# A token-mixing MLP block on one core: the first two tiles of x in one load, 64 words of w1 read on the second ring, and a new order of the work

## Chip, core and metric

The kernel runs on one core of one Trainium2 chip. The metric is the device time of one execution in microseconds (us). The median of four runs stands for the kernel. The profile is of one more execution; it lists the core's engines: PE (TensorE, matrix products; PEld is its weight load), DVE (VectorE), ACT (ScalarE), POOL (GpSimd) and SP (SyncE, which only issues DMAs here).

## What is computed

One batch, S = 2048 tokens, D = 512 features, F = 1792, all in bf16:

```python
h = _gelu(_layernorm(x, axis=-1) @ w1)                 # w1: 512 x 512
c = D // 4
g0 = ...   # the first quarter of h's columns, one token later
g1 = ...   # the second, one token earlier
g2 = ...   # the third, two tokens later
g3 = ...   # the fourth, two tokens earlier
hs = jnp.concatenate([g0, g1, g2, g3], axis=-1) @ w2   # w2: 512 x 512
x1 = x + hs
h2 = _gelu(_layernorm(x1, axis=-1) @ w3) @ w4          # w3: 512 x 1792, w4: 1792 x 512
return x1 + h2
```

Tokens that a shift would take from outside the sequence count as zero.

## The kernel before

The tokens are cut into 16 tiles of 128. All of x, x1 and the weights stay in on-chip memory. A tile passes through these steps:

- **Load.** `load` issues x by tiles (`x3`, or `x4-5` for two tiles in one DMA), w1, w2 and w4 in halves (`w1a`, `w1b`) and w3 whole. The order is the string `LOADS`. Everything goes on SP's queue, but for `x0@act`, which ScalarE issues on its own queue. Besides loads, SP's queue carries the DMA transposes (line 463) and 15 of the stores of the output.
- **Layernorm of layer 1** (`ln`). Mean and variance come from VectorE (lines 416 and 418) or, for tiles in `STAT_ACT`, from two passes on ScalarE (lines 395 and 400) and small VectorE steps. GpSimd raises the variance to the power -1/2 (`rstd`, line 423). The normalized tile is written by the engine that `NORM` names, VectorE by default (line 445), ScalarE (454) or GpSimd (457); for the last two a product of mean and rstd is made first (`nmr`, line 450, on the engine that `NMR` names).
- **Transpose.** Matrix products need features on partitions. Tiles in the script's `sa`, `sb` and `ty` steps are transposed on TensorE (line 490) and copied out of its accumulators (line 498) by the engines that `EVAC` names; the others by a DMA transpose on SP's queue. Numbers of 16 and above in `ty` and `tp` mean the second layernorm of tile number minus 16.
- **up1** with w1 and gelu (lines 626 and 641). Tiles are taken in groups, `GROUPS[1]`; `up1:6` in the script is group 6, not tile 6.
- **mix** (line 666): four products of shifted columns of h with w2 for one tile, then x1 on VectorE (lines 673, 677). Tile t needs h of tiles t-1 to t+1.
- **Layernorm of layer 2**, transposes, **up2** with w3 and gelu by groups `GROUPS[2]` (tiles 0-1, 2-5, 6-9, 10-11, 12-15), **down** with w4 (line 695), sum and store (lines 703 and 706).

Tile 0 takes a short way (`NAT`, `SPLIT`): only its mean is subtracted before the product (line 431, in two halves); it is turned in two halves (`sa`, `sb`), multiplied row-wise by the two halves of w1 (`ra` needs w1a, `rb` needs w1b; line 528), and scaled by rstd inside its gelu (line 569). The result is turned back (`th`, line 594) and copied (line 604).

TensorE's order is written out by hand in `SCRIPT`. `warm:9` at its head is nine products of zeros (line 720). Each other engine's order comes from a planner in `Program.order` and `Program.place`: each step gets a due time, counted back from TensorE's list, and at each moment the engine takes, of the steps that the planner holds ready, the one due first. `DUE` is where the count starts, `LAG` adds to the planned landing of loads and transposes, and `BIAS` moves single steps' due times by hand. The loads on a queue keep the order of `LOADS`. `emit` writes the instructions in the planned order and adds semaphore waits for true dependencies; instructions that the planner starts before `ENTRY` are moved ahead of the program's opening barrier.

```python
LOADS = """
x1 x2 tp2 x0@act w1a w1b x3 x4-5 tp5 w2a w2b x6-7 w3 tp17 w4a x8-10 w4b tp6 x11-12 tp1 tp16 x13-15
"""
```

Entries `tp` in `LOADS` that TensorE transposes are skipped; of these only `tp6` remains.

Of the kernel before, what the change touches and what calls it, by code (L numbers as in the profile page):

```python
# [6 lines left out]
P = 128  # L7
ACT_F = mybir.ActivationFunctionType
ALU = mybir.AluOpType
BF16 = mybir.dt.bfloat16  # L10
# [15 lines left out]
class Program:  # L26
# [2 lines left out]

    HOP = {"pe": 200.0, "dve": 155.0, "act": 220.0, "pool": 120.0, "sp": 70.0}  # L30
    LOOK = {"dve": 300.0, "act": 300.0}
    DUE = 164483.0
    BEGIN = {"sp": 30.0, "act": 150.0, "pe": 400.0, "dve": 150.0, "pool": 450.0}
    ENTRY = 1900.0
    COLD, RESTART = 4300.0, 800.0
    LAG = {"load": 750, "tp": 700}

    def __init__(self):
        self.ops = []
# [12 lines left out]
    def order(self):  # L52
# [58 lines left out]
        assert seen == len(self.ops), "cycle"  # L111
        if self.DUE:

            topo, left = [], [len(d) for d in preds]
            stack = [i for i, n in enumerate(left) if n == 0]
            while stack:
                i = stack.pop()
                topo.append(i)
                for j in succs[i]:
                    left[j] -= 1  # L120
                    if left[j] == 0:
                        stack.append(j)
            due, t = {}, self.DUE
            for op in self.ops:
# [12 lines left out]
        for op in self.ops:  # L137
            op.prio += BIAS.get(op.name, 0.0)
            if op.first is not None:
# [11 lines left out]
    def place(self, succs, order_only):  # L151
# [46 lines left out]
        def land(op):  # L198
            nonlocal moved, last
            if op.queue == "tp":  # L200
                at = max(clock + 500.0, op.start + 2450.0, last + 600.0) + self.LAG["tp"]
            elif op.name.startswith("out"):
                at = clock + 300.0
                self.total = max(self.total, at)
            else:
                moved += op.dur
                at = clock + 600.0 + min(600.0, 0.3 * moved) + (600.0 if op.dur > 1400.0 else 0.0)
                at += self.LAG["load"] if moved > 1200.0 else 50.0
            if op.queue != "tp":
# [47 lines left out]
        self.seq = out  # L257
        return out

GROUPS = {1: (1, 1, 1, 1, 2, 1, 4, 2, 2, 1), 2: (2, 4, 4, 2, 4)}  # L260
NORM = {0: "act", 3: "act", 7: "pool", 8: "act", 9: "pool", 10: "pool", 11: "pool", 12: "pool", 14: "act", 15: "act", 16: "pool", 18: "act", 19: "act", 24: "pool", 25: "act", 26: "pool", 27: "pool", 29: "pool", 30: "pool", 31: "act"}
EVAC = {0: "both", 1: "both", 2: "both", 4: "both", 8: "both", 9: "dve", 10: "dve", 11: "dve", 12: "dve", 13: "dve", 14: "dve", 16: "dve", 17: "dve", 19: "both", 20: "both", 21: "both", 22: "both", 23: "both", 24: "dve", 25: "both", 27: "both", 29: "both", 30: "both", 31: "both"}
STAT_ACT = (0, 7, 9, 12, 13, 15, 18, 21, 25, 29, 30)
TAIL = (256, 160, 96)
NMR = {0: "pool", 1: "pool", 3: "pool", 5: "pool", 6: "pool", 7: "pool", 8: "pool", 9: "pool", 11: "pool", 13: "pool", 14: "pool", 15: "pool", 16: "pool", 17: "pool", 18: "pool", 20: "pool", 21: "pool", 22: "pool", 26: "pool", 27: "pool", 28: "pool", 29: "pool", 31: "pool"}
NAT = (0,)
SPLIT = (0,)
CSPLIT = ()
HEV = {0: "dve", 4: "dve"}
BIAS = {}  # L270
LOADS = """
x1 x2 tp2 x0@act w1a w1b x3 x4-5 tp5 w2a w2b x6-7 w3 tp17 w4a x8-10 w4b tp6 x11-12 tp1 tp16 x13-15
"""
SCRIPT = """
warm:9 sa:0 sb:0 ty:1 ra:0 rb:0 ty:2 up1:1 th:0 up1:2 mix:0 ty:3 ty:5 mix:1 ty:4 up1:3-4 ty:16 mix:2 ty:17
mix:3 up2:0 mix:4 up1:5 down:1 down:0 mix:5 up1:6-7 mix:8 mix:6 up1:9 mix:9-10 up1:8 mix:7 mix:11 up2:1
mix:13 mix:15 up2:3 down:5 mix:12 up2:2 mix:14 down:2 down:4 down:3 down:6-8 down:11 down:9 up2:4 down:10
down:12-15
"""

def bass_standalone__mixer_s_mlp__prompt_kernel(nc, x, w1, w2, w3, w4, out):
# [3 lines left out]
    NT, DC, FC = S // P, D // P, F // P  # L285
    groups = {l: [(sum(GROUPS[l][:i]), n) for i, n in enumerate(GROUPS[l])] for l in GROUPS}
    NXN, NO, NPAIR, NOB, NJ = 16, 4, 3, 2, 4
# [8 lines left out]
    with ExitStack() as es:  # L296
        sb = lambda name, shape, dt: es.enter_context(nc.sbuf_tensor(name, shape, dt))
# [22 lines left out]
        warm = sb("warm", [P, 1], F32)  # L320
# [6 lines left out]
        pg = Program()  # L327
# [56 lines left out]
        def ln(layer, t):  # L384
# [3 lines left out]
            col = lambda a: a[:, q : q + 1]  # L388
            how = NORM.get(q, "dve")
            sign = -1.0 if q in NAT and how == "act" else 1.0  # L390
            if q in STAT_ACT:
                if layer == 1:
# [22 lines left out]
            else:  # L415
# [4 lines left out]
                       writes=[(("mv", q), 0), (("vpe", q), 0)], dur=75)  # L420
            var = vpe[:, q : q + 1] if q in STAT_ACT else mv[:, q, 1:2]
            pg.add("pool", f"rstd{q}",
# [3 lines left out]
            if q in NAT:  # L426
                assert how != "act" or q in STAT_ACT

# [18 lines left out]
            else:  # L447
                eng = NMR.get(q, "dve")
                pg.add(eng, f"nmr{q}",
# [17 lines left out]
        def pe_transpose(t, q, pair):  # L467
            layer = 1 if q < NT else 2
            how = EVAC.get(q, "act")
            if pair:  # L470
# [104 lines left out]
        def h_transpose(t):  # L575
            g = group_of[1, t]
            how = HEV.get(t, "act")
            k = NAT.index(t)
# [71 lines left out]
        def mm_mix(t):  # L650
# [20 lines left out]
            wr = [(("x1", t), 0)]  # L671
            if NT + t in STAT_ACT:
                f = lambda e: e.scalar_tensor_tensor(x1_sb[:, t, :], dst, 1.0, x_sb[:, t, :], ALU.mult, ALU.add,  # L673
# [57 lines left out]
        for step in SCRIPT.split():  # L731
            kind, n = step.split(":")
# [36 lines left out]
        for queue in queues.values():  # L769
            pg.line(queue)  # L770
        pg.order()
        emit(nc, es, pg)

def emit(nc, es, prog):

    engs = {"sp": nc.sync, "act": nc.scalar, "pe": nc.tensor, "dve": nc.vector, "pool": nc.gpsimd}
    sems = {e: es.enter_context(nc.semaphore("sem_" + e)) for e in ENGINES}
    ndma = 0
    for op in prog.seq:
        if op.queue is not None:  # L780
            op.stream = ("dma", ndma)
            sems[op.stream] = es.enter_context(nc.semaphore(f"sem_dma{ndma}"))
            ndma += 1
        else:
            op.stream = op.eng
    listed = nc.m.functions[0].blocks[0].instructions
    entry = next(i for i, ins in enumerate(listed) if type(ins).__name__ == "InstDrain")
    barrier = listed[entry:]
    late = [ins for ins in barrier
            if type(ins).__name__ == "InstEventSemaphore" and ins.engine != mybir.EngineType.Pool]  # L790
    early = [ins for ins in barrier if ins not in late]
    body = len(listed)
    ahead = body
    know = {e: {} for e in ENGINES}
    implied = {}
    count = {}
    last_write, readers = {}, {}
    for op in prog.seq:
        e = op.eng
        needs = {}  # L800

        def need(sv):
            if needs.get(sv[0], 0) < sv[1]:
                needs[sv[0]] = sv[1]

        for res, ver in op.reads:
            lw = last_write[res]
            assert lw[2] == ver, (op.name, res, ver, lw)
            need(lw)
        for res, ver in op.writes:  # L810
            if res in last_write:
                need(last_write[res])
            for sv in readers.get(res, ()):
                need(sv)
        if e == "pe":
            needs.pop("pe", None)
        k = know[e]
        for s, v in sorted(needs.items(), key=lambda sv: -sv[1]):
            if k.get(s, 0) >= v:
                continue  # L820
            engs[e].wait_ge(sems[s], v)
            for s2, v2 in implied[(s, v)].items():
                if v2 > k.get(s2, 0):
                    k[s2] = v2
            k[s] = max(k.get(s, 0), v)
        ins = op.fn(engs[e])
        if op.start < prog.ENTRY:
            ahead = len(listed)
        inc = 1 if op.queue is None else 16
        ins.then_inc(sems[op.stream], inc)  # L830
        val = count[op.stream] = count.get(op.stream, 0) + inc
        snap = dict(k)
        snap[op.stream] = max(snap.get(op.stream, 0), val)
        implied[(op.stream, val)] = snap
        for res, ver in op.reads:
            readers.setdefault(res, []).append((op.stream, val))
        for res, ver in op.writes:
            last_write[res] = (op.stream, val, ver)
            readers[res] = []
    listed[entry:ahead] = early + listed[body:ahead] + late  # L840
    for op in prog.seq:
        if op.name.startswith("out_dma"):
            nc.sync.wait_ge(sems[op.stream], 16)
# [28 lines left out]
```

## Time and profile before

| | |
|---|---|
| median of 4 runs | 135.64 us (135.14 to 136.1) |
| the profiled execution | 135.37 us |
| its span, first to last instruction | 134.1 us |
| busy: PE / ACT / DVE / POOL | 131.2 / 58.4 / 50.0 / 29.8 us |
| read from HBM, written to it | 6.82 MB, 2.10 MB |
| granted TensorE clock | 1.000 |

Times in the profile are counted from the span's start. A line of the timeline gives start, duration, engine, line of the kernel, operation, output and input by name, shape, number of instructions merged into the line and, in brackets, how long the engine had been idle and what ended that. "SPq" and "ACTq" are the issuing side of a DMA; its duration is the issue, not the transfer. The chain of waits is the sequence of work that ended last, each piece with its start and length.

### The profile page before, as it was taken

The numbers are of one execution on the slowest core, as the hardware profiler recorded it, in microseconds if no ns is written. First come the engines' busy times: TensorE is split into PE (matmuls) and PEld (weight loads), VectorE is DVE, ScalarE is ACT, GpSimd is POOL, SyncE is SP. The second block draws the span as 40 slices with busy tenths as digits, with TensorE's granted clock in tenths as the row PEclk, the third lists the DMA queues.
The fourth block names the chain that finished last, engine by engine and source line by source line (L and its number), as shares of the span: only waits on it lengthen the run. The fifth ranks groups of instructions, "written<-read, shape, count | busy, mean of one in ns | idle before, by whom it ended". The sixth has DMA issues, their size and how long they took to land.

```text
span 134.1 us, 2014 instructions
## 1 busy us (share of the span) xinstructions
PE 131.2 (98%) x789; PEld 71.4 (53%) x789; DVE 50.0 (37%) x134; ACT 58.4 (44%) x92; POOL 29.8 (22%) x68
## 2 busy tenths in 40 slices
PE   8899999999999999999999999999999999999994
PEld 3388687544656444478444444444444444444464
DVE  2789976756188920070070004232222200012223
ACT  5798359979635375547225553000000155520000
POOL 2444449892103850015010002100000000000000
DMA  4999998765453134100311000311111100001112
GB/s 142 311 377 397 350 300 232 62 112 98 98 107 94 39 80 83 34 0 16 67 39 39 0 0 0 78 39 44 39 41 66 50 0 0 0 5 39 39 39 78
DMA packets 21289, 12.19 MB, mean 91 GB/s; under 512 B 13856, under 2 KB 20768, under 8 KB 21280
## 3 DMA queue, kind: packets, MB, share of 16 engines
q1 hardware_dynamic: 20704, 11.80, 33.9%
q10 hardware_dynamic: 576, 0.26, 0.7%
q8 instruction: 6, 0.10, 0.3%
q14 instruction: 3, 0.02, 0.1%
HBM read 6.82 MB, written 2.10 MB: 66 GB/s over the span
## 4 chain that ended last, share of the span: by engine, by line
PE 94%; DMA 3%; SPq 1%; issue 0%; DVE 0%
PE y_ps L626 46%; PE o_ps L695 36%; PE o_ps L666 10%; DMA w_sb<-in_w_dram 3%; PE y_ps L490 1%; SPq L368 1%; PE y_ps L528 0%; SPq L377 0%; DVE o_sb L703 0%; PE o_ps L594 0%; SPq L857 0%
## 5 line engine op out<-in xcount | busy, mean ns | idle before, releaser
L626 PE MATMUL y_ps<-xnT,w_sb 128*128 128x512 bf16 (+2 forms) x424 | 63.6, 309 | 0.0
L626 PEld LDWEIGHTS y_ps<-xnT,w_sb 128*128 128x128 bf16 x424 | 38.3, 98 | 24.8
L641 ACT ACTIVATE h2T<-y_ps 128x1024 bf16<-128x1024 f32 (+1 forms) x29 | 28.6, 993 | 48.8 <-PE y_ps L626 48.6
L695 PE MATMUL o_ps<-w_sb,h2T 128*128 128x512 bf16 (+3 forms) x252 | 49.1, 355 | 0.0
L695 PEld LDWEIGHTS o_ps<-w_sb,h2T 128*128 128x128 bf16 x252 | 23.5, 98 | 24.7
L703 DVE TENSOR_TENSOR o_sb<-o_ps,x_sb 128x512 bf16<-128x512 f32 (+3 forms) x18 | 11.4, 632 | 46.9 <-PE o_ps L695 46.9
L423 POOL TENSOR_TENSOR rstd<-mv,neghalf 128x1 f32<-128x1 f32 x21 | 11.5, 549 | 23.1 <-DVE mv L418 14.2
L666 PE MATMUL o_ps<-w_sb,hT 128*128 128x512 bf16 x64 | 15.8, 379 | 0.0
L416 DVE BATCH_NORM_STATS2 st<-x_sb 128x6 f32<-128x512 bf16 x21 | 14.1, 678 | 3.6 <-DMA x_sb<-in_x_dram 3.4
L423 POOL TENSOR_TENSOR rstd<-vpe,neghalf 128x1 f32<-128x1 f32 x11 | 6.0, 548 | 29.3 <-DVE vpe L412 29.2
L673 DVE SCALAR_TENSOR_TENSOR x_sb<-o_ps,x_sb 128x512 bf16<-128x512 f32 x5 | 3.4, 684 | 19.0 <-PE o_ps L666 19.0
L641 ACT ACTIVATE hT<-y_ps 128x512 bf16<-128x512 f32 (+1 forms) x10 | 8.1, 806 | 5.1 <-PE y_ps L626 5.0
L666 PEld LDWEIGHTS o_ps<-w_sb,hT 128*128 128x128 bf16 x64 | 6.0, 98 | 5.8
L677 DVE TENSOR_TENSOR x_sb<-o_ps,x_sb 128x512 bf16<-128x512 f32 x11 | 7.5, 683 | 3.8 <-PE o_ps L666 3.6
L457 POOL TENSOR_SCALAR xn_buf<-x_sb,rstd,nmr 128x512 bf16<-128x512 bf16 x11 | 8.4, 765 | 0.8 <-DVE nmr L450 0.4
L400 ACT ACTIVATE junk<-x_sb 128x512 bf16<-128x512 bf16 x11 | 6.9, 624 | 2.2 <-DVE x_sb L673 2.2
L454 ACT ACTIVATE xn_buf<-x_sb,nmr,rstd 128x512 bf16<-128x512 bf16 x8 | 6.3, 807 | 1.2 <-POOL nmr L450 1.1
L445 DVE TENSOR_SCALAR xn_buf<-x_sb,mv,rstd 128x512 bf16<-128x512 bf16 x12 | 5.3, 443 | 2.9 <-POOL rstd L423 2.6
L395 ACT ACTIVATE junk<-x_sb 128x512 bf16<-128x512 bf16 x6 | 3.7, 624 | 0.7 <-DMA x_sb<-in_x_dram 0.7
L720 PE MATMUL o_ps<-zeros 128*128 128x512 bf16 x9 | 3.6, 581 | 0.4 <-DVE zeros L347 0.4
L418 DVE BATCH_NORM_AGGREGATE mv<-st 128x2 f32<-128x9 f32 x21 | 3.8, 189 | 0.3
L450 POOL TENSOR_SCALAR nmr<-mv,rstd 128x1 f32<-128x1 f32 x13 | 3.4, 263 | 0.7
(34 smaller groups left out, 28.0 us busy)
## 6 DMA issues: line engine op xcount, KB each, us to landing
out_dram<-o_sb SPq DMA_DIRECT2D x15, 128.0 KB, 1.7
w_sb<-in_w_dram SPq DMA_DIRECT2D x1, 1792.0 KB, 9.5
w_sb<-in_w_dram SPq DMA_DIRECT2D x2, 896.0 KB, 11.8
w_sb<-in_w_dram SPq DMA_DIRECT2D x4, 256.0 KB, 4.7
x_sb<-in_x_dram SPq DMA_DIRECT2D x3, 256.0 KB, 5.3
x_sb<-in_x_dram SPq DMA_DIRECT2D x2, 384.0 KB, 9.6
x_sb<-in_x_dram SPq DMA_DIRECT2D x3, 128.0 KB, 2.6
xnT<-xn_buf SPq DMA_TRANSPOSE x24, 2.5
```

What stands on the lines that cost most here:

```text
L400: (lambda d: (lambda e: e.activation(d, src, ACT_F.Square, accum_out=sums[:, q, 1:2])))(junk[:, b, :]),
L416: pg.add("dve", f"bnst{q}", lambda e: e.bn_stats(st9[:, q, 0:6], src), reads=rs, writes=[(("st", q), 0)], dur=605)
L423: lambda e: e.tensor_tensor(col(rstd), var, neghalf[:], ALU.pow),
L445: lambda e: e.tensor_scalar(dst, src, mv[:, q, 0:1], rstd[:, q : q + 1], ALU.subtract, ALU.mult),
L454: f = lambda e: e.activation(dst, src, ACT_F.Identity, bias=nmr[:, q : q + 1], scale=rstd[:, q : q + 1])
L457: f = lambda e: e.tensor_scalar(dst, src, rstd[:, q : q + 1], nmr[:, q : q + 1], ALU.mult, ALU.add)
L626: ins = e.matmul(y_ps[:, p, W * i : W * (i + 1)], wsb[:, dc, P * fc : P * (fc + 1)], src[:, dc, P * t0 : P * t0 + W], start=(dc == 0), sto ...
L641: (lambda d, s: (lambda e: e.activation(d, s, ACT_F.Gelu_apprx_tanh)))(dst, ysrc),
L666: ins = e.matmul(dst, hT[:, j, c0 : c0 + P], w2_sb[:, j, :], start=(j == 0), stop=(j == DC - 1))
L677: f = lambda e: e.tensor_tensor(x1_sb[:, t, :], dst, x_sb[:, t, :], ALU.add)
L695: ins = e.matmul(dst, h2T[:, fc, P * t : P * (t + 1)], w4_sb[:, fc, cs], start=(fc == 0), stop=(fc == FC - 1))
L703: (lambda d, c: (lambda e: e.tensor_tensor(o_sb[:, oi, c], d, x1_sb[:, t, c], ALU.add)))(dst, cs),
```

## The change

- `LOADS` begins with `x0-1`, one DMA of two tiles on SP's queue. `x0@act` is gone. Later loads come in another order and in other pieces: x8 ahead of w3, then x10, x9, x7 and x6 singly ahead of w4, and x11 to x15 singly behind it.
- ScalarE's queue gets one DMA instead of x0: for 16 rows (every eighth of 128) and the four row blocks of w1 it reads two neighbouring bf16 values, so 64 reads of 4 bytes, into a small buffer `seen` that nothing uses. It is emitted just ahead of ScalarE's first instruction. SP waits for it at the program's very end.
- `SCRIPT`, `GROUPS[1]`, `NORM`, `EVAC`, `STAT_ACT`, `NMR`, `BIAS`, `DUE` and one entry of `LAG` are replaced. In `HEV` only the entry of tile 0 has an effect, and it stays. `TAIL`, `NAT`, `SPLIT` and `GROUPS[2]` stay.

```diff
-    DUE = 164483.0
+    DUE = 94375.3
...
-    LAG = {"load": 750, "tp": 700}
+    LAG = {"load": 450, "tp": 700}
...
-GROUPS = {1: (1, 1, 1, 1, 2, 1, 4, 2, 2, 1), 2: (2, 4, 4, 2, 4)}
-NORM = {0: "act", 3: "act", 7: "pool", 8: "act", 9: "pool", 10: "pool", 11: "pool", 12: "pool", 14: "act", 15: "act", 16: "pool", 18: "act", 19: "act", 24: "pool", 25: "act", 26: "pool", 27: "pool", 29: "pool", 30: "pool", 31: "act"}
-EVAC = {0: "both", 1: "both", 2: "both", 4: "both", 8: "both", 9: "dve", ...}
-STAT_ACT = (0, 7, 9, 12, 13, 15, 18, 21, 25, 29, 30)
+GROUPS = {1: (1, 1, 1, 1, 1, 1, 4, 1, 2, 1, 2), 2: (2, 4, 4, 2, 4)}
+NORM = {0: "act", 4: "pool", 9: "pool", 11: "pool", 12: "pool", 13: "pool", 14: "pool", 15: "act", 19: "pool", 20: "pool", 21: "act", 22: "act", 23: "act", 25: "act", 28: "pool", 29: "act", 31: "act"}
+EVAC = {0: "dve", 2: "both", 3: "dve", 8: "both", 9: "dve", ..., 16: "both", 17: "dve", ...}
+STAT_ACT = (0, 5, 7, 8, 9, 13, 21, 22, 28, 30)
...
-BIAS = {}
+TOUCH = ("act", ('w1',))
+BIAS = {"bnag14": -172.25, "bnag2": -591.918, "bnag28": -353, "bnst6": 1934.91, "msq0": -541.481, "ssq4": -586, "vpe0": -295.453, "vpe9": 895}
 LOADS = """
-x1 x2 tp2 x0@act w1a w1b x3 x4-5 tp5 w2a w2b x6-7 w3 tp17 w4a x8-10 w4b tp6 x11-12 tp1 tp16 x13-15
+x0-1 x2 w1a w1b x3 tp17 tp4 x4-5 w2b w2a x8 tp4 w3 tp17 x10 x9 tp1 x7 x6 w4a w4b x15 x12 x14 tp0 x11 x13
 """
 SCRIPT = """
-warm:9 sa:0 sb:0 ty:1 ra:0 rb:0 ty:2 up1:1 th:0 up1:2 mix:0 ty:3 ty:5 mix:1 ty:4 up1:3-4 ty:16 mix:2 ty:17
-mix:3 up2:0 mix:4 up1:5 down:1 down:0 mix:5 up1:6-7 mix:8 mix:6 up1:9 mix:9-10 up1:8 mix:7 mix:11 up2:1
-mix:13 mix:15 up2:3 ...
+warm:10 sa:0 sb:0 ty:1 ra:0 rb:0 ty:2 up1:1 th:0 up1:2 ty:3 mix:0 up1:3 mix:1 ty:4 mix:2 ty:5 up1:4 ty:16
+up1:5 ty:17 mix:3 up2:0 mix:4 down:1 up1:6 down:0 mix:5 up1:8 up1:7 mix:6-7 up1:9 mix:9 mix:8 up1:10 mix:10
+up2:1 mix:11 mix:15 up2:2 ...
 """
...
+        n = len(TOUCH[1])
+        seen = sb("seen", [16, n * DC, 2], BF16)
+        rows = lambda w: w.rearrange("(c p) f -> p c f", p=P)[0 : P : 8, 0:DC, 0:2]
+        words = [(seen[:, DC * i : DC * (i + 1), :], rows({"w1": w1, "w2": w2}[k])) for i, k in enumerate(TOUCH[1])]
+        emit(nc, es, pg, words)
...
+        if e == TOUCH[0] and not touched:
+            for i, (to, frm) in enumerate(words):
+                touched.append(es.enter_context(nc.semaphore(f"sem_touch{i}")))
+                engs[e].dma_start(to, frm).then_inc(touched[-1], 16)
...
+    for sem in touched:
+        nc.sync.wait_ge(sem, 16)
```

More of the change, by code (lines that the diff above doesn't have):

```diff
@@ L258, in place @@
         return out
-GROUPS = {1: (1, 1, 1, 1, 2, 1, 4, 2, 2, 1), 2: (2, 4, 4, 2, 4)}
-NORM = {0: "act", 3: "act", 7: "pool", 8: "act", 9: "pool", 10: "pool", 11: "pool", 12: "pool", 14: "act", 15: "act", 16: "pool", 18: "act", 19: "act", 24: "pool", 25: "act", 26: "pool", 27: "pool", 29: "pool", 30: "pool", 31: "act"}
-EVAC = {0: "both", 1: "both", 2: "both", 4: "both", 8: "both", 9: "dve", 10: "dve", 11: "dve", 12: "dve", 13: "dve", 14: "dve", 16: "dve", 17: "dve", 19: "both", 20: "both", 21: "both", 22: "both", 23: "both", 24: "dve", 25: "both", 27: "both", 29: "both", 30: "both", 31: "both"}
-STAT_ACT = (0, 7, 9, 12, 13, 15, 18, 21, 25, 29, 30)
+GROUPS = {1: (1, 1, 1, 1, 1, 1, 4, 1, 2, 1, 2), 2: (2, 4, 4, 2, 4)}
+NORM = {0: "act", 4: "pool", 9: "pool", 11: "pool", 12: "pool", 13: "pool", 14: "pool", 15: "act", 19: "pool", 20: "pool", 21: "act", 22: "act", 23: "act", 25: "act", 28: "pool", 29: "act", 31: "act"}
+EVAC = {0: "dve", 2: "both", 3: "dve", 8: "both", 9: "dve", 10: "both", 11: "both", 13: "dve", 15: "dve", 16: "both", 17: "dve", 18: "dve", 20: "both", 22: "dve", 27: "both", 29: "both", 30: "dve", 31: "both"}
+STAT_ACT = (0, 5, 7, 8, 9, 13, 21, 22, 28, 30)
 TAIL = (256, 160, 96)
-NMR = {0: "pool", 1: "pool", 3: "pool", 5: "pool", 6: "pool", 7: "pool", 8: "pool", 9: "pool", 11: "pool", 13: "pool", 14: "pool", 15: "pool", 16: "pool", 17: "pool", 18: "pool", 20: "pool", 21: "pool", 22: "pool", 26: "pool", 27: "pool", 28: "pool", 29: "pool", 31: "pool"}
+NMR = {0: "pool", 4: "pool", 5: "pool", 6: "pool", 7: "pool", 10: "pool", 14: "pool", 15: "pool", 16: "pool", 17: "pool", 18: "pool", 19: "pool", 20: "pool", 22: "pool", 25: "pool", 27: "pool", 28: "pool", 31: "pool"}
 NAT = (0,)
@@ L268 @@
 CSPLIT = ()
-HEV = {0: "dve", 4: "dve"}
-BIAS = {}
+HEV = {0: "dve", 1: "dve", 3: "dve", 4: "dve", 6: "dve"}
+TOUCH = ("act", ('w1',))
+BIAS = {"bnag14": -172.25, "bnag2": -591.918, "bnag28": -353, "bnst6": 1934.91, "msq0": -541.481, "ssq4": -586, "vpe0": -295.453, "vpe9": 895}
 LOADS = """
-x1 x2 tp2 x0@act w1a w1b x3 x4-5 tp5 w2a w2b x6-7 w3 tp17 w4a x8-10 w4b tp6 x11-12 tp1 tp16 x13-15
+x0-1 x2 w1a w1b x3 tp17 tp4 x4-5 w2b w2a x8 tp4 w3 tp17 x10 x9 tp1 x7 x6 w4a w4b x15 x12 x14 tp0 x11 x13
 """
 SCRIPT = """
-warm:9 sa:0 sb:0 ty:1 ra:0 rb:0 ty:2 up1:1 th:0 up1:2 mix:0 ty:3 ty:5 mix:1 ty:4 up1:3-4 ty:16 mix:2 ty:17
-mix:3 up2:0 mix:4 up1:5 down:1 down:0 mix:5 up1:6-7 mix:8 mix:6 up1:9 mix:9-10 up1:8 mix:7 mix:11 up2:1
-mix:13 mix:15 up2:3 down:5 mix:12 up2:2 mix:14 down:2 down:4 down:3 down:6-8 down:11 down:9 up2:4 down:10
-down:12-15
+warm:10 sa:0 sb:0 ty:1 ra:0 rb:0 ty:2 up1:1 th:0 up1:2 ty:3 mix:0 up1:3 mix:1 ty:4 mix:2 ty:5 up1:4 ty:16
+up1:5 ty:17 mix:3 up2:0 mix:4 down:1 up1:6 down:0 mix:5 up1:8 up1:7 mix:6-7 up1:9 mix:9 mix:8 up1:10 mix:10
+up2:1 mix:11 mix:15 up2:2 mix:12 down:2 down:4 mix:14 up2:3 mix:13 down:3 down:6-7 up2:4 down:10-11 down:8
+down:14 down:5 down:9 down:12-13 down:15
 """
@@ L771, in bass_standalone__mixer_s_mlp__prompt_kernel, with emit @@
         pg.order()
-        emit(nc, es, pg)
-def emit(nc, es, prog):
+        n = len(TOUCH[1])
[3 more added lines that the diff above has]
+        emit(nc, es, pg, words)
+def emit(nc, es, prog, words):
     engs = {"sp": nc.sync, "act": nc.scalar, "pe": nc.tensor, "dve": nc.vector, "pool": nc.gpsimd}
@@ L797, in emit @@
     last_write, readers = {}, {}
+    touched = []
     for op in prog.seq:
```

## The prediction, made before the changed kernel was run

> **What bounds the kernel now.** The page first, then the chain of waits, because PE fills almost the whole span:
>
> ```profile
> span 134.1 us, 2014 instructions
> ...
> PE 131.2 (98%) x789; PEld 71.4 (53%) x789; DVE 50.0 (37%) x134; ACT 58.4 (44%) x92; POOL 29.8 (22%) x68
> ```
>
> ```profile
> 1.47 4.54 DMA w_sb<-in_w_dram
> 6.00 0.05 issue
> 6.05 0.61 PE y_ps L528 x2
> 6.66 0.22 PE y_ps L490 x4
> ...
> 7.77 0.22 PE o_ps L594 x4
> ...
> 16.24 6.11 PE y_ps L626 x56
> ...
> 24.11 6.04 PE o_ps L695 x28
> ```
>
> From 6.05 on the chain is PE alone, to 132.25: 126.2 us of products that the change leaves in number. The end is therefore set by when PE gets going, and by whether it ever waits afterwards. What it waits for at first is one load, w1b. The timeline gives the arrivals, as the ends of idle times:
>
> ```profile
> 2.51 0.69 DVE L416 BATCH_NORM_STATS2 st<-x_sb 128x6 f32<-128x512 bf16 x1 [2.12 <-DMA x_sb<-in_x_dram]
> 2.84 0.63 ACT L395 ACTIVATE junk<-x_sb 128x512 bf16<-128x512 bf16 x1 [0.73 <-DMA x_sb<-in_x_dram]
> 3.60 0.91 ACT L431 ACTIVATE xn_buf<-x_sb,mv 128x256 bf16<-128x256 bf16 x2
> 4.25 0.82 PE L490 MATMUL y_ps<-ident,xn_buf 128*128 128x128 bf16 x8 [0.19 <-ACT xn_buf L431]
> 5.32 0.11 PEld L528 LDWEIGHTS y_ps<-w_sb,xnT 128*128 128x128 bf16 x2 [0.43 <-DMA w_sb<-in_w_dram]
> 5.90 0.55 POOL L423 TENSOR_TENSOR rstd<-vpe,neghalf 128x1 f32<-128x1 f32 x1 [0.64 <-DVE vpe L412]
> 6.05 0.11 PEld L528 LDWEIGHTS y_ps<-w_sb,xnT 128*128 128x128 bf16 x2 [0.61 <-DMA w_sb<-in_w_dram]
> 6.76 0.69 ACT L569 ACTIVATE hn<-y_ps,rstd 128x512 bf16<-128x512 f32 x1 [0.94 <-PE y_ps L528]
> ```
>
> x1 is there at 2.5, x0 at 2.8, w1a at 5.3, w1b at 6.05. Why w1 takes so long is in the table of stages (columns: stage, length, busy PE, PEld, DVE, ACT, POOL, clock, DMA share, GB/s):
>
> ```profile
> 1.60:2.60 1.00, 1.00 (x4) 0.34 (x3) 0.09 (x1) 0.50 (x2) 0.08 (x2) 1.00 0.91 315
> 2.60:3.40 0.80, 0.80 (x3) 0.26 (x2) 0.77 (x3) 0.56 (x2) 0.00 (x0) 1.00 0.67 134
> 3.40:4.20 0.80, 0.66 (x3) 0.15 (x1) 0.69 (x3) 0.77 (x4) 0.56 (x1) 1.00 0.71 114
> 4.20:6.20 2.00, 1.53 (x11) 0.69 (x12) 1.53 (x7) 1.57 (x5) 0.85 (x2) 1.00 1.08 376
> ```
>
> Once x0 to x2 are through, the rate falls to 134 and 114 GB/s for 1.6 us and then stands at 376. In the trace's packet records 14 packets of w1a, begun between 3.34 and 3.78, take 360 to 855 ns where the others take 46; 8 of the first packets of x, from 1.10 on, show the same (365 to 611 ns), while none of w2, w3 and w4 takes over 286. So the first reads of w1 stall nearly all DMA engines once. The 1.6 us moved 198 KB, worth 0.53 us at 376 GB/s: 1.1 us are lost.
>
> **The change, part by part.** *x0-1 in one load.* By 2.2 us both rings together had moved the 262 kB of two tiles (111 GB/s from 1.0 to 1.6 is 67, then 315). Loads land some 0.5 us after their last packet (x2's last starts at 2.6; it lands 2.6 after its issue at 0.54, so at 3.1). So x0-1 lands at 2.7: x0 0.1 earlier, x1 0.2 later. The lower bound is 2.5 (x1 alone now); the upper 3.8, if the whole stall moves ahead of it. I take 2.7, nearer to the row of x0 now. SP issues one DMA less ahead of w1 (0.41 us), which is hidden, as its ring is never empty of x before 2.6.
>
> *The touch.* It replaces an issue of 0.37 us on ACT at 0.21, ahead of a table load; its issue costs nothing new. Nobody waits for it until SP's last wait. What it brings lies between nothing (w1b at 6.0) and the 1.1 us (w1b at 4.9). I take the full amount: x0's packets on this ring start at 1.67, so the touch reads w1 more than a microsecond before w1a's packets come (2.73). The Trainium skill, "DMA: Bandwidth & Descriptors", section "Rules for kernel authors", speaks against it: transfers under 64 KB pay mostly overhead and should be merged, and this one has 256 bytes. By that rule alone the touch is waste, w1b stays at 6.05 and the gelu of tile 0 at 6.76, and of the sum below 0.1 us remains: 135.6. The stages above show a cost that the rule does not speak of.
>
> *Tile 0's way, with x0-1 at 2.7, all of 2.84's chain 0.12 earlier.* The mean ends at 3.45, the centred halves at 3.93 and 4.39. PE takes them at 4.15 and 4.5: the tenth warm product fits, since the eighth and ninth start 0.27 apart (3.41, 3.68) and the array is free at 4.1. DVE now copies both halves out (EVAC 0), 0.33 after each start and 0.29 long: 4.77 and 5.12. Products of rows: 4.95 to 5.38 and to 5.81, against 6.66 now, if w1b is there by 5.4. Then the gelu needs rstd: ACT no longer copies a half (0.38), so its squares follow at 4.42 and end at 5.2, the variance at 5.4, POOL 5.48 to 6.03, the gelu at 6.07 instead of 6.76. PE has tile 2's transposes and up1 of tile 1 meanwhile (0.22 and 0.89, to 6.92), and the turned-back h (line 594) can start at 6.07 + 0.69 + 0.16 = 6.92 instead of 7.61. **0.7 us gained**, two limits meeting.
>
> *What must follow.* From 8 to 14 us DVE is busy 5.58 of 6, so it can swallow the lead. Tiles 0 to 5, 16 and 17 cost DVE 0.88 less for tile 5's statistics (now ACT) and 0.33 more for its small steps; the copies come out even (1.97 against 1.98). So DVE has 0.5 us less, about the lead's size; ACT takes 1.6 more against 0.8 less for tile 3. I count nothing lost, between 0.7 lost and 0.1 gained (the first mix takes 0.98 in the chain, the others 0.86). *Groups:* a pair of tiles less, two singles more: 2 x 0.89 against 1.75, 0.03 lost. *DUE* shifts due times together and is free; *LAG* acts through the order alone. *Later loads:* x6 now ends behind x8, x9 and x10 besides all that came up to w3's end (14.05): 393 kB at the 393 GB/s of 8 to 14 us, so 1.0 us more, less the 1.1: 13.9.
>
> Sum: 0.7 + 0.1 - 0.03 = 0.8 us. The profiled execution (134.1 in the span, 1.3 around it) would be 134.6; it lay 0.27 under the median, so the median goes from 135.64 to 134.8.
>
> **The rivals.** *The wait is moved, not removed.* The 64 reads pass the same 16 DMA engines as x0-1, and their stall falls on x0-1's second half. For it: two rings together ran at 315 GB/s, one later at 376, so the rings share. At the full 1.1 us x0-1 lands at 3.8 and the gelu of tile 0 starts at 7.2, 0.4 late: 136.0; at half of it, 0.14 early: 135.5. Against it: the stall is waiting, not moving, and touch and x may wait at once. About 135.6, no change.
>
> *Group 6 comes too early (slower).* The script now runs up1 of tiles 6-9 right behind down:1, at 16.24 - 0.8 + 6.1 + 0.9 + 3.0 = 25.4; before, the first group of four ran at 31.0. Its four DMA transposes pass SP's queue behind w4:
>
> ```profile
> 9.44 1.89 SPq L377 DMA_DIRECT2D w_sb<-in_w_dram x1
> 15.36 1.88 SPq L463 DMA_TRANSPOSE xnT<-xn_buf  x1
> 17.29 1.09 SPq L368 DMA_DIRECT2D x_sb<-in_x_dram  x2
> 19.25 12.63 SPq L463 DMA_TRANSPOSE xnT<-xn_buf  x7
> ```
>
> The first landed 6.4 us after its issue (21.8, just behind w4b at 21.3), the fourth at 27.9. At that pace PE stands 2.5 us at 25.4, or 1.4 with all loads 1.1 earlier: 136.2 to 137.3. It decides once the fourth lands after 26.2. Against it: these transposes waited for tiles that came at 18.8 behind w4a, and now all four x are in by 13.9, leaving 6 us for statistics that take 1.3 to 2 per tile over two engines; w4b lands near 20.2, and four transposes 1.3 apart are through by 24.
>
> **How the numbers follow.** Forecast 0.48, the moved wait 0.26, the early group 0.26. A change of 0.5% (0.7 us) is about what a measurement of this kernel can tell from no change; 134.8 lies just past it. PE's idle time between 4.25 and 6.66 is 1.1 us (2.41 less 1.3 of work), x0-1 could come 0.3 earlier, the first mix has 0.1: no more than 1.6 is to be had, so the low end is 134.0. The high end takes in most of the early group: 136.9. Faster 0.48, same 0.26, slower 0.26.
>
> **What would show it.** Right: line 528 starts by 5.0 and does not wait for w_sb a second time; the rate stays above 300 GB/s from 2.6 to 4.2; line 594 starts near 6.9 and up2's first 56 products near 15.4. Wrong: DVE and ACT waiting for x past 3.2; a PE wait for xnT from a DMA transpose near 25; DVE named before PE between 8 and 16.

## The result, and the profile after

The changed kernel takes 136.36 us (median of 31 runs, 135.78 to 137.67); the kernel before takes 135.56 us (50 runs). The ratio is 1.006, with a 95% interval of 1.0046 to 1.0073: the change makes the kernel 0.8 us slower, where 0.8 us faster was forecast. The profiled execution took 136.51 us, 135.1 of it in the span (before: 135.37 and 134.1). Line numbers of the helper functions are one higher than before (528 is now 529, 626 is 627). The ratios in this document leave out the executions whose mean granted clock lay below 1.000, which are five of the ten of `a_old_loads_tp` and two of the nine of `a_tp_first`, two kernels of the experiments.

The page of the kernel after:

```profile
span 135.1 us, 2049 instructions
...
PE 132.4 (98%) x806; PEld 71.9 (53%) x806; DVE 51.9 (38%) x136; ACT 57.2 (42%) x89; POOL 27.6 (20%) x62
```

The timeline of its start, in the order of the lines shown of before:

```profile
2.98 0.69 DVE L417 BATCH_NORM_STATS2 st<-x_sb 128x6 f32<-128x512 bf16 x1 [2.62 <-DMA x_sb<-in_x_dram]
5.44 0.13 PEld L529 LDWEIGHTS y_ps<-w_sb,xnT 128*128 128x128 bf16 x2 [0.16 <-DMA w_sb<-in_w_dram]
5.79 0.55 POOL L424 TENSOR_TENSOR rstd<-vpe,neghalf 128x1 f32<-128x1 f32 x1
6.17 0.11 PEld L529 LDWEIGHTS y_ps<-w_sb,xnT 128*128 128x128 bf16 x2 [0.60 <-DMA w_sb<-in_w_dram]
6.88 0.69 ACT L570 ACTIVATE hn<-y_ps,rstd 128x512 bf16<-128x512 f32 x1 [0.80 <-PE y_ps L529]
7.40 0.69 DVE L417 BATCH_NORM_STATS2 st<-x_sb 128x6 f32<-128x512 bf16 x1 [1.21 <-DMA x_sb<-in_x_dram]
7.74 0.39 PE L595 MATMUL o_ps<-ident,hn 128*128 128x128 bf16 x4
8.34 1.07 PE L627 MATMUL y_ps<-xnT,w_sb 128*128 128x128 bf16 x16 [0.22 <-DVE xnT L499]
9.59 0.40 PE L491 MATMUL y_ps<-ident,xn_buf 128*128 128x128 bf16 x4 [0.18 <-DVE xn_buf L446]
```

PE still waits for both halves of w1, to 5.44 and 6.17 (before 5.32 and 6.05). The product that turns tile 0's h back, which should have moved from 7.61 to 6.92, stands at 7.74. The table of stages says why (stage, length, busy PE, PEld, DVE, ACT, POOL, clock, DMA share, GB/s):

```profile
1.60:2.60 1.00, 1.00 (x4) 0.37 (x3) 0.00 (x0) 0.51 (x2) 0.09 (x2) 1.00 0.88 292
2.60:3.40 0.80, 0.80 (x4) 0.25 (x3) 0.41 (x1) 0.42 (x1) 0.00 (x0) 1.00 1.04 164
3.40:4.20 0.80, 0.80 (x3) 0.29 (x2) 0.77 (x3) 0.77 (x4) 0.21 (x1) 1.00 0.61 106
4.20:6.20 2.00, 1.87 (x13) 0.75 (x12) 1.81 (x8) 1.65 (x5) 1.32 (x3) 1.00 0.99 339
```

The stall is where it was: 164 and 106 GB/s, against 134 and 114. The 64 reads had landed by 2.68, their packets between 1.8 and 2.3; and yet 12 packets of w1a, begun from 2.98 to 4.05, took 481 to 1142 ns.

So the gain is missing. The loss is in the chain of waits of the same execution:

```profile
2.18 5.20 DMA x_sb<-in_x_dram
...
7.40 0.69 DVE st L417
...
17.27 6.11 PE y_ps L627 x56
...
24.25 3.09 PE o_ps L696 x14
27.34 3.45 PE y_ps L627 x16
```

up2's first 56 products start at 17.27, 1.03 later than before, while PE's work ahead of them is the same set of steps in another order. Here x3 came at 7.4, and DVE stood 1.21 us in front of its statistics. They stand ahead of the copy of tile 2 in the new order of DVE, and PE lacks that copy at 8.34 and tile 3 at 9.59. It looks like the cause, but it belongs to this execution: the last of the 16 DMA engines finished x3 at 7.37, the fifteenth at 6.49. One more profile of the very same kernel has x3 in time and shows another loss of nearly the same size, and that one is found in every profile of this order in which nothing earlier hides it.

### The profile page after: what moved, and what is told of

It reads as the page before. It is cut to its first block, busy times and chain, and to the rows that moved or that the text cites. A ratio compares the mean times of both kernels' runs of the same rounds, so it can differ in the third digit from the quotient of the medians.

```text
span 135.1 us, 2049 instructions
## 1 busy us (share of the span) xinstructions
PE 132.4 (98%) x806; PEld 71.9 (53%) x806; DVE 51.9 (38%) x136; ACT 57.2 (42%) x89; POOL 27.6 (20%) x62
## 4 chain that ended last, share of the span: by engine, by line
PE 92%; DMA 4%; DVE 1%; POOL 0%; issue 0%; DVEq 0%
PE y_ps L627 44%; PE o_ps L696 36%; PE o_ps L667 10%; DMA x_sb<-in_x_dram 4%; PE y_ps L491 1%; DVE st L417 1%; POOL rstd L424 0%; DVE xn_buf L446 0%; DVE o_sb L704 0%; DVE xnT L499 0%; DVE mv L419 0%; DVEq L831 0%
## 5 line engine op out<-in xcount | busy, mean ns | idle before, releaser
L424 POOL TENSOR_TENSOR rstd<-mv,neghalf 128x1 f32<-128x1 f32 x22 | 12.3, 562 | 31.3 <-DVE mv L419 29.5
L417 DVE BATCH_NORM_STATS2 st<-x_sb 128x6 f32<-128x512 bf16 x22 | 14.8, 677 | 4.0 <-DMA x_sb<-in_x_dram 3.8
L678 DVE TENSOR_TENSOR x_sb<-o_ps,x_sb 128x512 bf16<-128x512 f32 x12 | 8.2, 685 | 14.3 <-PE o_ps L667 14.2
L424 POOL TENSOR_TENSOR rstd<-vpe,neghalf 128x1 f32<-128x1 f32 x10 | 5.5, 551 | 26.8 <-DVE vpe L413 26.8
L401 ACT ACTIVATE junk<-x_sb 128x512 bf16<-128x512 bf16 x10 | 6.3, 627 | 10.6 <-DVE x_sb L674 10.6
L446 DVE TENSOR_SCALAR xn_buf<-x_sb,mv,rstd 128x512 bf16<-128x512 bf16 x15 | 6.5, 435 | 6.0 <-POOL rstd L424 5.5
L674 DVE SCALAR_TENSOR_TENSOR x_sb<-o_ps,x_sb 128x512 bf16<-128x512 f32 x4 | 2.8, 692 | 11.4 <-PE o_ps L667 11.4
L458 POOL TENSOR_SCALAR xn_buf<-x_sb,rstd,nmr 128x512 bf16<-128x512 bf16 x9 | 6.9, 767 | 0.5 <-DVE nmr L451 0.4
L455 ACT ACTIVATE xn_buf<-x_sb,nmr,rstd 128x512 bf16<-128x512 bf16 x7 | 5.5, 806 | 3.2 <-DVE nmr L451 2.9
L721 PE MATMUL o_ps<-zeros 128*128 128x512 bf16 x10 | 4.4, 631 | 0.4 <-DVE zeros L348 0.4
L396 ACT ACTIVATE junk<-x_sb 128x512 bf16<-128x512 bf16 x6 | 3.8, 631 | 1.2 <-DMA x_sb<-in_x_dram 1.2
L491 PE MATMUL y_ps<-ident,xn_buf 128*128 128x128 bf16 x32 | 3.1, 222 | 0.2 <-DVE xn_buf L446 0.2
(34 smaller groups left out, 26.9 us busy)
```

The lines of the kernel that those rows point to most:

```text
L401: (lambda d: (lambda e: e.activation(d, src, ACT_F.Square, accum_out=sums[:, q, 1:2])))(junk[:, b, :]),
L417: pg.add("dve", f"bnst{q}", lambda e: e.bn_stats(st9[:, q, 0:6], src), reads=rs, writes=[(("st", q), 0)], dur=605)
L424: lambda e: e.tensor_tensor(col(rstd), var, neghalf[:], ALU.pow),
L446: lambda e: e.tensor_scalar(dst, src, mv[:, q, 0:1], rstd[:, q : q + 1], ALU.subtract, ALU.mult),
L455: f = lambda e: e.activation(dst, src, ACT_F.Identity, bias=nmr[:, q : q + 1], scale=rstd[:, q : q + 1])
L458: f = lambda e: e.tensor_scalar(dst, src, rstd[:, q : q + 1], nmr[:, q : q + 1], ALU.mult, ALU.add)
```

## The experiments

Ratios are to the kernel before, which ran beside each on the same chip (medians 135.50 to 135.56 us), and stand on 5 to 12 executions of each edited kernel. All edits but two are to the changed kernel ("after"); `b_` marks edits to the kernel before.

The planned sequence is changed by a small helper, called after the planner, which puts one step just behind another:

```python
def behind(pg, *pairs):
    for name, other in pairs:
        op = pg.seq.pop(next(i for i, o in enumerate(pg.seq) if o.name == name))
        pg.seq.insert(1 + next(i for i, o in enumerate(pg.seq) if o.name == other), op)
```

**Is it the loads?** Four kernels: the changed one without the touch; the changed one with the old two loads of x0 and x1 and without the touch; and, into the kernel before, each of the two alone.

`a_no_touch`:

```diff
-        emit(nc, es, pg, words)
+        emit(nc, es, pg, [])
```

> The changed kernel without its 64-word read; x0-1 still comes in one load on SP's queue and ScalarE's queue is empty until the end; the order of the work is the same instruction for instruction. Theory 1 (the order is at fault: it needs x3 at 5.8 us and the loads cannot bring it): w1b still lands near 6.1, x3 near 6.4 to 7.4, time 135.9 to 136.4, ratio to before 1.003 to 1.006. Theory 2 (the 64 reads put one DMA engine behind, and x3's last engine is 0.9 us later than the other fifteen for that reason): the sixteen landings of x3 stand within 0.8 us as before, x3 is there by 6.5, time 135.4 to 135.6, ratio 0.998 to 1.001. Theory 3 (the touch does warm w1, only not enough): w1b lands later than 6.13 by 0.3 us or more, time 136.7 or above, ratio 1.008.

Measured: 136.26 us, 1.0051 [1.0036, 1.0066].

`a_old_loads`:

```diff
+        two.fn = lambda e: e.dma_start(x_sb[:, 1:2, :], xt[:, 1:2, :])      # SP: x1 alone
+        one = Op("dma_x0_alone", "act", lambda e: e.dma_start(x_sb[:, 0:1, :], xt[:, 0:1, :]), ...)
-        emit(nc, es, pg, words)
+        emit(nc, es, pg, [])
```

> The changed kernel's order of the work, but its first loads as before: x1 alone on SP's queue, x0 alone on ScalarE's, no 64-word read. All other loads as changed. Theory 1 (the order): x3 lands at 6.4 as before, and the order still holds PE for the difference to 5.8, 0.3 to 0.6 us: time 135.7 to 136.1, ratio 1.001 to 1.004. Theory 2 (the loads are the whole loss): x3 at 6.4 and w2 by 8.8 let the order keep what it was planned to gain: time 135.3 to 135.6, ratio 0.998 to 1.000. If the time stays at 136.4 the loads are off the case and the order alone loses 0.8 us.

Measured: 136.12 us, 1.0045 [1.0023, 1.0067].

`b_x01`:

```diff
+        two.fn = lambda e: e.dma_start(x_sb[:, 0:2, :], xt[:, 0:2, :])      # SP: x0 and x1
+        pg.seq.remove(one)                                                 # ScalarE: x0's load
```

> The kernel before, in its own order, with one part of the change alone: x0 and x1 in one load on SP's queue, nothing on ScalarE's. Theory 1: x0 lands about when it did (2.8 to 3.0), x1 0.5 later than before (2.9), the rest of the loads as before; time 135.5 to 135.8, ratio 0.999 to 1.002. Theory 2 (the single load or the idle second queue puts one engine behind): x3's last landing moves from 6.4 to about 7.4, its landings spread over 1.7 us; the old order needs x3 only in its fourth tile, behind the first mix, so 0.2 to 0.8 us are lost: ratio 1.002 to 1.006.

Measured: 135.66 us, 1.0008 [0.9995, 1.0021]. x0-1 landed at 2.97 here too.

`b_touch`:

```diff
+        if op.name == "dma_x0":
+            nc.scalar.dma_start(*word).then_inc(touch, 16)    # the 64 words of w1, right behind x0
```

> The kernel before, in its own order, with the other part alone: the 64-word read of w1 on ScalarE's queue, issued right behind x0 there. Theory 1 (the reads neither warm w1 nor harm): long packets of w1a between 3 and 4.3 us as before, w1b at 6.0, time 135.5 to 135.7, ratio 0.999 to 1.001. Theory 2 (the reads put one engine behind): x3's landings spread over 1.5 us or more, last near 7.3, time 135.8 to 136.3, ratio 1.002 to 1.005. Prediction's step (the reads take the stall of w1 on themselves): no long packets of w1a, w1b by 5.2, time 134.9 to 135.3, ratio 0.995 to 0.998.

Measured: 135.61 us, 1.001 [0.9994, 1.0026]. With the touch at work the two slow stages still read

```profile
2.60:3.40 0.80, 0.80 (x3) 0.25 (x2) 0.69 (x1) 0.40 (x1) 0.00 (x0) 1.00 1.08 121
3.40:4.20 0.80, 0.80 (x3) 0.15 (x1) 0.76 (x2) 0.77 (x4) 0.51 (x1) 1.00 0.45 129
```

and 11 packets took 486 to 1113 ns. What follows: neither the touch nor the single load, alone or together, makes a difference beyond some 0.3 us, which is what these intervals leave open. The 0.6 to 0.8 us are lost in the rest of the change, the new order of the work and of the later loads, with the old first loads as with the new.

**Where in the order?** `a_again` is the changed kernel, unedited, profiled once more.

> The changed kernel unchanged, one more profile. If its late DMA engine (the sixteenth landing of x3 0.9 us behind the fifteenth, at 7.4 us) belongs to this kernel, it is there again, and PE again waits 0.7 us between 8 and 10 us. If it is chance, x3 lands by 6.6 and group 6 waits for its fourth transpose near 26.9 instead; the time is 136.0 to 136.5 in either case, because the second bound stands behind the first.

Its span is 134.9 us. x3 landed at 6.37, up2's first products started at 16.25 (before: 16.24), so up to there nothing is lost and nothing won. Then, in its timeline of PE:

```profile
23.20 3.18 PE L696 MATMUL o_ps<-w_sb,h2T 128*128 128x512 bf16 x14
26.93 3.61 PE L627 MATMUL y_ps<-xnT,w_sb 128*128 128x512 bf16 x16 [0.55 <-DMA xnT<-xn_buf]
```

and in its chain:

```profile
6.33 8.85 DMA x_sb<-in_x_dram
...
21.69 0.70 SPq L464
22.39 0.04 issue
22.44 4.35 DMA xnT<-xn_buf
26.79 0.14 issue
26.93 3.61 PE y_ps L627 x16
```

This is group 6, up1 of tiles 6 to 9, right behind down of tile 1. PE is through with down at 26.22 (in the chain its 14 products take 3.02) and stands until 26.93, when the last of four DMA transposes has come: 0.71 us, of the 0.8 that this span is longer than that before. The profiles of two more kernels with this order, where no late x hides it, show the same transpose as the releaser: PE waited 0.38 us (to 27.02) in `a_no_touch`, where w1b had come 0.5 us later, and 0.59 us (to 26.87) in `a_old_loads`; from their chains:

```profile
22.53 4.36 DMA xnT<-xn_buf
...
27.02 3.61 PE y_ps L627 x16
```

```profile
22.24 4.50 DMA xnT<-xn_buf
26.74 0.14 issue
26.87 3.61 PE y_ps L627 x16
```

Three kernels, and group 6 starts within 0.15 us, whatever the loads at the start did. In the profiled execution of after it started at 27.34 in the chain; the transpose had landed at 26.73 there, so of the 1.03 us that PE came late it would have lost about half anyway. The two delays stand one behind the other, and the later one decides.

Why the transposes are so late is on SP's queue. The timeline of `a_again` has

```profile
7.55 4.12 SPq L378 DMA_DIRECT2D w_sb<-in_w_dram  x2
11.71 6.08 SPq L369 DMA_DIRECT2D x_sb<-in_x_dram  x5
17.84 12.79 SPq L464 DMA_TRANSPOSE xnT<-xn_buf  x8
```

Five x of 128 KB (655 kB) are issued between w4 and the first transpose. The first one landed 6.0 us after its issue, where the median of the 24 in this kernel is 2.5. The four landed at 23.87, 25.22, 25.71 and 26.79. The fourth is that of tile 9, the only one of the four that POOL normalizes:

```profile
20.39 0.77 POOL L458 TENSOR_SCALAR xn_buf<-x_sb,rstd,nmr 128x512 bf16<-128x512 bf16 x1 [0.36 <-DVE nmr L451]
```

Its input was ready at 21.16, but it was issued at 22.44 only, right behind the issue of the third (20.74 to 22.39). From 7.55 to 23.70 SP issues without a pause; what the fourth waited for last was its place in the queue.

**The transposes first, or group 6 later?** Two ways to take the wait away. `a_old_loads_tp` has the old loads and `a_tp_first` the new ones; in both x13 to x15 go behind the four transposes.

```diff
+        behind(pg, ('dma_x15', 'tp9'), ('dma_x14', 'dma_x15'), ('dma_x13', 'dma_x14'))
```

> The run with the old first loads (x1 on SP, x0 on ScalarE, no 64-word read), and besides it the loads of x15, x14 and x13 moved on SP's queue from ahead of the four DMA transposes of tiles 6 to 9 to behind them (393 kB, 1.0 us at 393 GB/s). Theory 1 (two bounds in a row: the first loads decide when PE gets to group 6, and the fourth transpose decides when group 6 may start): with the first bound gone, the second one is what is left; the fourth transpose lands near 25.7 instead of 26.7, PE takes group 6 near 26.3 without the 0.6 us wait, time 135.4 to 135.6, ratio 0.998 to 1.001 against 1.0045 of the run without the move. Theory 2 (the fourth transpose waits for its normalized tile, not for its place in the queue): no change, ratio 1.0045.

> The changed kernel with its own first loads and its 64-word read, and only the loads of x15, x14 and x13 moved behind the four DMA transposes of tiles 6 to 9. Theory 1 (two bounds in a row): PE gets to group 6 at 27.3 for reasons that lie before 10 us, and the transposes are there by then anyway; landing them 1 us earlier brings nothing: ratio 1.004 to 1.006. Theory 2 (the transposes alone are the loss): time 135.6 to 135.8, ratio 1.001 to 1.002.

Measured: 1.0082 [1.0055, 1.0109] and 1.0077 [1.005, 1.0103]. Every expected ratio missed, as none had foreseen a further loss, but the first half of the mechanism is there. In `a_old_loads_tp` the four transposes landed at 22.87 to 25.16, the fourth 1.58 earlier than in `a_old_loads` (26.74), with three x fewer ahead of it. Its tile was ready at 20.64 and 20.79, so it was not the tile that held it. The timeline of PE and ACT reads

```profile
26.16 3.62 PE L627 MATMUL y_ps<-xnT,w_sb 128*128 128x512 bf16 x16
...
26.44 0.63 ACT L396 ACTIVATE junk<-x_sb 128x512 bf16<-128x512 bf16 x1 [3.40 <-DMA x_sb<-in_x_dram]
...
31.88 0.81 ACT L455 ACTIVATE xn_buf<-x_sb,nmr,rstd 128x512 bf16<-128x512 bf16 x1 [2.78 <-POOL nmr L451]
32.60 1.00 ACT L642 ACTIVATE hT<-y_ps 128x1024 bf16<-128x1024 f32 x1
33.75 1.02 PE L667 MATMUL o_ps<-w_sb,hT 128*128 128x512 bf16 x3 [0.95 <-ACT hT L642]
```

Group 6 starts at 26.16 without a wait. Now x13 is late: ACT stands 3.40 us for it, the steps of tile 13 and of tile 15 behind them run late, and group 6's second gelu (line 642) stands on ACT behind the normalization of tile 15 (line 455), so that PE's next mix waits to 33.75. The wait was moved 7 us down the line and became 0.4 us longer than that of `a_again` (0.95 in place of 0.55). The profile of `a_tp_first` shows the same, only longer:

```profile
26.51 3.62 PE L627 MATMUL y_ps<-xnT,w_sb 128*128 128x512 bf16 x16
...
28.37 0.63 ACT L396 ACTIVATE junk<-x_sb 128x512 bf16<-128x512 bf16 x1 [4.98 <-DMA x_sb<-in_x_dram]
...
35.68 1.34 PE L667 MATMUL o_ps<-w_sb,hT 128*128 128x512 bf16 x3 [2.53 <-ACT hT L642]
```

Right behind this wait of 2.53 us the granted clock reads 0.56 from 36 to 38 us and 0.58 from 38 to 40, where it had read 1.00 before and does again from 40 on. With the 0.95 us of `a_old_loads_tp` it stays at 1.00.

`a_down0` leaves the queue alone. It takes down of tile 0 ahead of group 6, and puts the mix of tile 5 behind group 8, so that the mix need not wait for group 6's gelu:

```diff
+        behind(pg, ('down0_0', 'x1_4'), ('mix5', 'up1_8_0'))
```

It was run with the new loads, without the touch, and with the old loads and no touch.

> The changed kernel with its first loads and its 64-word read, and one thing moved on TensorE: down of tile 0 runs ahead of up1 of group 6 (tiles 6 to 9) instead of behind it, and the mix of tile 5 behind up1 of group 8 so that it does not wait for group 6's gelu. No product is added or taken away; the transposes are issued as before. Theory 1 (group 6 stands too early: its fourth transpose lands near 26.8 whatever comes first, and PE is ready for it near 26.2): PE has down of tile 0 to do until 29.3, the wait of 0.4 to 0.7 us at 26.9 is gone, time 135.3 to 135.8, ratio 0.998 to 1.002 against 1.006. Theory 2 (the loss is in the first loads alone): ratio stays at 1.004 to 1.006.

> The same, without the 64-word read: x0-1 in one load on SP's queue, nothing on ScalarE's. With the wait at group 6 out of the way, a difference in the first loads comes through to the end. If the read shortens w1's way (w1b landed at 6.1 and 5.9 with it, 6.4 without it, in one profile each), this run is 0.3 to 0.5 us above the one with the read; if it does nothing, they agree within 0.2 us; if it does harm (the late engine), this one is 0.3 us or more below.

> The same move on TensorE with the old first loads (x1 on SP's queue, x0 on ScalarE's, no 64-word read). Theory 1: 135.2 to 135.6, ratio 0.997 to 1.001, so that with the wait at group 6 gone the new order is as good as the old one and no better, since the products of tile 0 begin when w1 is there in either. If the new loads are worth anything by themselves, this run is above the two others; if they cost something, below them.

Measured: 135.61 us, 1.0 [0.9983, 1.0017]; 135.68 us, 1.0002 [0.9987, 1.0018]; 135.58 us, 0.9994 [0.9972, 1.0016]. The chain of `a_down0`:

```profile
16.61 6.11 PE y_ps L627 x56
...
23.58 6.11 PE o_ps L696 x28
29.70 5.20 PE y_ps L627 x32
```

The fourth transpose landed at 27.45 there; PE has 28 products of down instead of 14 until 29.7 and never notices. All of the loss is gone by these two moves on PE. The second took away no wait of its own: in `a_again` the mix of tile 5 starts at 33.40, as soon as down of tile 0 is through (30.38 + 3.02). These three also give the cleanest test of the first loads, since nothing behind the start hides it now: 135.61 with the touch, 135.68 without, 135.58 with the old loads, all alike within the 0.2 to 0.3 us of their intervals.

**Is the stall w1's?** `a_w2_first` puts w1 behind w2, to see whether the long packets stay at their time or go with w1.

```diff
+        behind(pg, ('dma_w1a', 'dma_w2a'), ('dma_w1b', 'dma_w1a'))
```

> The changed kernel with the two halves of w2 loaded ahead of the two of w1, a look at where the long packets fall; tile 0's product waits for w1 some 1.4 us longer, so the time is 1 us or more above 136.4 and is not the point. If the first reads of w1 stall (as the prediction had it, for whatever reason the 64 words do not help), the packets of w2 at 2.9 us are short and those of w1 near 4.3 us are long. If the stall belongs to the place in the queue or the moment (anything behind x2 at 3 to 4.2 us), the packets of w2 are the long ones and w1 passes at full rate.

One execution, 139.67 us, slower as expected, but not by the wait for w1 alone:

```profile
8.16 1.89 PE L529 MATMUL y_ps<-w_sb,xnT 128*128 128x512 bf16 x4 [2.72 <-DMA w_sb<-in_w_dram]
```

The granted clock reads 0.50 to 0.52 from 8 to 11 us, right behind this wait. The stages below lie ahead of it, at 1.00. The edit moved w1 behind x3 and x4-5 as well, so that these came first in the queue. The stages:

```profile
2.60:3.40 0.80, 0.80 (x3) 0.26 (x2) 0.43 (x1) 0.43 (x1) 0.00 (x0) 1.00 0.64 143
3.40:4.20 0.80, 0.80 (x3) 0.30 (x2) 0.77 (x3) 0.77 (x4) 0.23 (x1) 1.00 0.85 221
```

Nine packets of 392 to 964 ns lie between 2.6 and 4.4 us, as before, but by the bytes ahead of them they are of x3 and x4-5 (the first perhaps still of x2); w1's packets begin at 6.29 here. So the stall is not w1's, and a read of w1 ahead of time can't take it. Whether it goes with the moment or with the place behind the first x no run tells apart.

## Why the prediction was wrong, point by point

- **The touch: the step that failed, for the gain.** The sum took the whole 1.1 us, on the reading that "the first reads of w1 stall nearly all DMA engines once". It brought 0: the product with w1b starts at 6.17 against 6.05, and the times are 135.61 us with the touch, 135.68 without. Over the profiles w1b landed at 5.76 to 6.29 with the touch and w1 in its usual place (five) and at 5.42 to 7.15 without it (seven). That only packets of w1 were long at 3.3 to 3.8 in the trace of before was so because only w1 was in the queue then; `a_w2_first` shows others in its place. In that one trace time and tensor can't be told apart at the start, and that none of w4 takes over 286 ns was misread: nine of w4b's last packets, begun from 19.35 to 20.26 beside the first DMA transpose, take 0.9 to 1.8 us. "Nothing" stood as the other end, and the rule of the Trainium skill that was weighed there ("DMA: Bandwidth & Descriptors", "Rules for kernel authors": small transfers pay mostly overhead and should be merged) called the touch waste, as it proved. The trace agrees with the rule: the touch's 256 bytes took 2.48 us from issue to landing, x2's 131 kB 2.73.
- **x0-1 in one load.** Predicted at 2.7, landed at 2.96: tile 0 comes 0.1 later than before, not 0.1 earlier. Worth nothing in time (`b_x01`: 1.0008), as w1b ends the wait. Nor did the tenth product of zeros fit: the eighth, ninth and tenth start at 3.39, 3.81 and 4.24 in the profile after, 0.43 apart for the 0.27 of before, and tile 0's transposes at 4.67 for 4.15. w1 hid that too.
- **Tile 0's way.** Its other limit, rstd, was ready at 6.34 (5.79 + 0.55), so the gelu at 6.07 was 0.27 too early even had w1b come in time. As it was, w1b ruled: gelu at 6.88, turning back at 7.74. The 0.7 us were 0. The sum's other gain, 0.1, has behind it only the upper bound of a term that the text counts as nothing, the first mix; in the chain after that mix takes 0.97, for 0.98 before. The low end was summed too far by 0.1 as well (1.1, 0.3 and 0.1 are 1.5, not 1.6), which changes nothing.
- **"Nothing lost" on DVE.** In `a_again` so: up2's first products at 16.25. But the new order has less slack for a late x3, as the profile after shows: 1.03 us, more than the bound of 0.7 lost. Since group 6 would have waited for its transposes anyway, it cost that execution only 0.4 us more than the transposes did.
- **The moved wait.** It was not the case; nothing was removed that could be moved, though this rival's time (135.6) is what the changed loads alone give.
- **Group 6 too early, given 0.26: this was the case, and the step that failed for the loss.** The sum put this wait at nothing; it was 0.7 us in `a_again`. The rival named the place (behind down of tile 1), the mechanism (four transposes behind loads on SP's queue) and the point from which it decides (a fourth landing after 26.2; it was 26.79 in `a_again`). That the median, 136.36, falls into its price of 136.2 to 137.3 is partly luck: the price was made of 0.8 us gained and a wait of 1.4 to 2.5, where nothing was gained and the wait was 0.7. What kept its chance down was the sentence "all four x are in by 13.9 ... four transposes 1.3 apart are through by 24". The four x were in at 15.54 in `a_again` (x6, the last), 1.6 later, of which the 1.1 us at the start that were not saved are the larger part. w4b landed at 21.67, for 20.2. And w4b was counted as the last load ahead of the transposes, with the five x in the new `LOADS` left out, though the list stood in the diff: the last of them landed at 23.38, and the first transpose 0.49 behind it, at 23.87. The 6 us for the statistics were about right: the last tile was normalized at 21.16, 5.6 behind x6. The transposes landed rather closer than 1.3 us apart (1.35, 0.49, 1.08).
- **What would show it.** The wait for w_sb a second time, the rate below 300 GB/s and DVE named before PE between 8 and 16 came out on the wrong side in the profile after, the PE wait for xnT from a DMA transpose (at 26.9, for "near 25") in that of `a_again`.

With the right terms the sum was there to be made: nothing gained at the start, PE at 26.2, the transpose at 26.8: 0.6 to 0.7 us lost, 136.3.

## What to carry to other kernels

Price a DMA transpose by everything that stands ahead of it on its queue, read from the new order of the queue and not from the last big load, and by the time its own input is ready; then compare it with the moment at which the new script wants it. A stall seen in one trace can't be put down to a tensor before a run with another tensor in that place. And where two delays stand one behind the other, one profile names only the later: profile the same kernel twice before the chain of one execution is taken for the cause.

## What was not expected of the hardware

- Between 2.6 and 4.4 us after the start 9 to 12 packets take 0.4 to 1.1 us in the profiles of after and `b_touch` (of w1a) and of `a_w2_first` (of x3 and x4-5). The rate in these 1.6 us differs from execution to execution: 164 and 106 GB/s in the first profile of after, 210 and 252 in that of `a_again`, the same kernel. In `a_old_loads_tp`, without the touch, no packet there takes over 0.35 us, and w1b landed at 5.42, the earliest of all. What stalls them stays open; no run here tells it.
- The last of the 16 DMA engines can be 0.9 us behind the fifteenth (x3 after: 6.49 and 7.37) and in another execution of the same kernel hardly at all (6.33 and 6.37), where w4b's last engine is then 0.9 us behind (20.75 and 21.67).
- A DMA transpose behind five x loads on the same queue landed 6.0 us after its issue, against a median of 2.5.
- In both profiles with a mean granted clock of 0.988 the low clock, 0.50 to 0.58 for some 3 to 4 us, stands right behind PE's longest wait (2.53 us in `a_tp_first`, 2.72 us in `a_w2_first`). That the wait brings it on is not shown: no run changes the length of a wait alone.
